# Attention then a squared-ReLU feed-forward layer on one core: the second batch weighs v in float32, w_out is converted in pieces of 384 columns, the reciprocal is placed late in its slot, and the conversion of w_in follows another timetable

## The chip, the core and the metric

The kernel runs on one core of a Trainium2 chip. The metric is device time in microseconds (us) of one execution; of each kernel several executions are timed and the median is given. TensorE (PE, with PEld for its weight loads) multiplies matrices, VectorE (DVE) and ScalarE (ACT) work element by element, GpSimd (POOL) does so too, and SyncE (SP) issues the DMA transfers from one queue in order. Each engine takes its own instructions in program order.

## The reference

```python
def _attn_ref(q, k, v, g_q, g_k):                 # batch 8, 12 heads, 448 rows, head width 64
    q_n, k_n = rmsnorm(q, g_q), rmsnorm(k, g_k)   # x / sqrt(mean(x*x) + 1e-6) * g
    scores = 1/sqrt(64) * q_n @ k_n.T
    attn = exp(scores - scores.max(-1))
    attn = attn / (attn.sum(-1) + 1e-9)
    return attn @ v

def _moe_ref(x, w_in, w_out, s, b):               # x: 3584 x 768, w_in: 768 x 2048, w_out: 2048 x 768
    r = maximum(x @ w_in, 0)
    return (s * (r * r) + b) @ w_out              # x is the attention's output, heads side by side
```

w_in and w_out come as float64, the rest of the large inputs as float32.

## The kernel before

**Pairs, chunks and slots.** Two heads of one batch entry make a pair; there are 48 pairs, 6 to a batch (`NP = 6`). A pair has `W = 8` score chunks: for each of its two heads, four chunks of up to 128 keys by 448 queries. A hand-written loop runs over slots `s_`, from `FIRST = -22` on, and in slot `s_` the engines get, in a fixed order: the two score matmuls of chunk `s_` (`score_t`, L405 and L408), its exponential on ACT (`exponent`), the jobs that a table lists for this slot (`at(slot, function, ...)`), a score matmul for chunk `s_ + 10` that is only there to find the row maxima (`score`, L367, and on DVE `maximum`, L378), and the weighing of v with chunk `s_ - 2` (`weigh`, L464). All engines are ordered by this loop (`manual_schedule`). Slots below 0 are the prologue, slots 0 to 47 the first batch, 48 to 95 the second, and so on to 383.

**float32 and fp32r.** Matmuls on float32r operands go through PE in one pass. To keep precision an operand is split in a high part (rounded to fp32r, by a cast on ACT) and a low part (the remainder, by a subtraction), and products of parts are added up. For the first batch (`p < NP`) `weigh` instead multiplies plain float32: the exponential is written to a float32 tile `e` (L420) and one float32 matmul with `vf` does the chunk, without any split. For the other pairs the exponential stays in PSUM (L424), `split_e` casts it to `ah` (L432, ACT), `split_e_lo` subtracts to `al` (L445, DVE), `split_v` splits v (L297 on ACT, L298 on POOL), and a chunk takes three matmuls, or two where the fourth key chunk of 64 rows packs both parts in one tile: 22 for the 8 chunks of a pair.

**Filler.** From the end of slot 60 on the feed-forward matmuls of the batch before (`ffn_in`, L180: 16 units of 18) stand between the score matmuls, 6 to a slot (`FILL`), so that each batch of 48 slots carries 288 of them. At each change of batch, in slots 48*b + 11 to 48*b + 13, `split_x` splits the six x tiles of the batch just finished (L513 on ACT, L514 on DVE).

**Per pair besides.** `scale` and `split_kq` prepare q and k of the pairs from 6 on (L329, L351, L352 on POOL, L330 on DVE). `take` moves the weighed values out of PSUM, `gather` brings the row sums by DMA into `zt`, `divide` step 0 (slot `8p + 13`) adds 1e-9 and takes the reciprocal on DVE (L489, L490), steps 1 and 2 spread it by DMA, step 3 multiplies on POOL (L505).

**The weights.** `load_double` makes the two parts of a float64 piece: a DMA into `w64`, four integer or float operations on DVE (L125, L128, L130, L133) that put a float32 word together in `wa`, a square on ACT (L126) that serves one of them, a cast of the high part on ACT (L136) and the subtraction of the low part on POOL (L139). w_in has 24 pieces of 128 x 512. `PACE` lists the slot in which each piece's conversion starts, and a piece takes five slots; two pieces are loaded ahead, and the load of a further one stands three slots after each start:

```python
PACE = (-18, -10, *range(1, 61, 5), *range(61, 91, 3))
at(s_ + n, convert, n)      # n = 0..4; convert stands behind the slot's other DVE work
at(s_ + 3, load_piece)
```

**The last stage.** After the slots come the last batch's feed-forward units and the conversion of w_out, 48 pieces of 128 x 256 (`WO = 256`), in a loop over `m` with three pieces a step; a step's casts and subtractions follow four steps later, since w_out takes over w_in's buffers quarter by quarter. `squares` loads three tiles of 128 rows of relu values (1 MB each), squares them on ACT (L682), scales them on DVE (L683) and splits them (L687 ACT, L688 DVE); `ffn_out` multiplies them with w_out (L700), the first three tiles together, then one by one. A PSUM bank of a feed-forward unit comes free when ACT's relu (L197, `rectify`) has read it, and the first three output tiles need six such banks. SP is ordered by the scheduler there, and `ffn_out` as well.

## Time and profile before

| | |
|---|---|
| median of 3 runs | 1547.24 us (1546.6 to 1549.03) |
| profiled execution | 1545.13 us, of which the span from the first to the last instruction is 1543.3 us |
| busy share of the span | PE 95%, PEld 87%, DVE 58%, ACT 53%, POOL 49% |
| mean granted TensorE clock | 0.979 |
| DMA | 230.86 MB, mean 150 GB/s |
| chain that ended last | PE 29%, DVE 3%, DMA 2% of the span (the rest of the span is not in it) |

PE is busy nearly all of the time on the average, but not in every stage: the page's 40 slices show PE between 0.6 and 0.9 in the first seven of them and dips again about two thirds of the way. The views to read are therefore those by stage: the busy time of each engine in a stretch, the waits in it, and the order of instructions in time.

### The profile page before, as it was taken

Reading aid. Unit: us, or ns where it says so; the run is one execution under the profiler, and the core shown is the slowest. Engines: PE = TensorE matmul, PEld = TensorE weight load, DVE = VectorE, ACT = ScalarE, POOL = GpSimd, SP = SyncE. Lnnn points to the kernel's source line nnn. Section 1 sums busy time; section 2 is a strip of 40 time slices with the busy share of each in tenths; the row PEclk is TensorE's granted clock in tenths of the full one; section 3 lists DMA queues with packets and bytes.
Section 4 is the critical chain, followed back from the end, with each engine's and each line's share of the span. In section 5 each row is a group of like instructions: output and inputs, shape, how many; then the busy total and the mean of one; then the engine's idle time right before and its main releaser. Section 6 shows DMA issues by size and latency. Waiting matters only on the chain. (4 is left out here: it accounts for less than half of the span.)

```text
span 1543.3 us, 21847 instructions
## 1 busy us (share of the span) xinstructions
PE 1459.3 (95%) x7380; PEld 1343.6 (87%) x7380; DVE 892.6 (58%) x1399; ACT 812.5 (53%) x1522; POOL 748.6 (49%) x611
## 2 busy tenths in 40 slices
PE   7886799999999999999999999997899999999998
PEld 6654688899899899899889889996899999999998
DVE  5989998766666766766666664389532222222210
ACT  4766676666666666766766666346342222222210
POOL 6799898777667667667677753135500000000000
PEclk8998899999999999999999999998899999999999
DMA  4477676566566566656666651466243323323300
GB/s 118 133 198 217 183 231 201 161 193 202 159 189 191 173 193 193 183 166 201 189 172 194 188 164 56 125 218 199 82 140 91 97 75 88 101 76 86 103 21 31
DMA packets 218751, 230.86 MB, mean 150 GB/s; under 512 B 72912, under 2 KB 193744, under 8 KB 218640
## 3 DMA queue, kind: packets, MB, share of 16 engines
q1 hardware_dynamic: 218640, 229.47, 50.3%
q8 instruction: 58, 0.95, 0.3%
q14 instruction: 53, 0.43, 0.1%
HBM read 177.21 MB, written 40.84 MB: 141 GB/s over the span
## 5 line engine op out<-in xcount | busy, mean ns | idle before, releaser
L180 PE MATMUL ph<-x,wih 128*128 128x448 f32 x1536 | 493.1, 368 | 0.0
L424 ACT ACTIVATE st<-st 128x448 f32<-128x448 f32 x336 | 176.5, 525 | 261.2 <-PE st L408 244.6
L180 PEld LDWEIGHTS ph<-x,wih 128*128 128x128 f32 x1536 | 290.8, 189 | 24.0 <-issue 0.2
L378 DVE TENSOR_REDUCE nmx<-sh 112x1 fp32r<-112x448 f32 x384 | 237.1, 620 | 126.4 <-PE sh L367 121.1
L180 PE MATMUL ph<-x,wil 128*128 128x448 f32 x768 | 282.2, 367 | 0.0
L700 PE MATMUL po<-woh,gh 128*128 128x384 f32 x896 | 230.9, 337 | 12.5 <-ACT gh L687 7.8
L700 PE MATMUL po<-wol,gh 128*128 128x384 f32 x896 | 230.5, 337 | 4.1 <-POOL wol L139 4.1
L700 PE MATMUL po<-woh,gl 128*128 128x384 f32 x896 | 229.1, 336 | 0.0
L464 PE MATMUL av<-ah,vs 128*128 128x448 f32 x672 | 194.7, 371 | 6.1 <-DVE ah L445 3.2
L445 DVE TENSOR_TENSOR al<-st,ah 128x448 fp32r<-128x448 f32 x252 | 155.5, 617 | 44.6 <-ACT ah L432 26.0
L432 ACT CAST ah<-st 128x448 fp32r<-128x448 f32 x336 | 179.6, 535 | 2.0
L700 PEld LDWEIGHTS po<-woh,gh 128*128 128x128 f32 x896 | 163.4, 189 | 13.9 <-ACT gh L687 8.1
L367 PE MATMUL sh<-ka,qa 128*112 128x448 f32 x384 | 147.8, 387 | 23.0 <-POOL ka L351 8.4
L700 PEld LDWEIGHTS po<-wol,gh 128*128 128x128 f32 x896 | 163.4, 189 | 5.5 <-POOL wol L139 5.5
L700 PEld LDWEIGHTS po<-woh,gl 128*128 128x128 f32 x896 | 162.9, 189 | 0.5 <-DVE gl L688 0.5
L405 PE MATMUL st<-qa,ka 128*128 128x448 f32 (+1 forms) x384 | 159.2, 414 | 0.5 <-ACT e L420 0.5
L180 PEld LDWEIGHTS ph<-x,wil 128*128 128x128 f32 x768 | 145.2, 189 | 11.4
L351 POOL TENSOR_TENSOR ka<-kq,ka 64x448 fp32r<-64x448 f32 x84 | 100.4, 1196 | 108.4 <-ACT ka L348 97.3
L464 PEld LDWEIGHTS av<-ah,vs 128*128 128x128 f32 x672 | 127.5, 191 | 20.3 <-DVE al L445 3.5
L408 PE MATMUL st<-qb,kb 128*128 128x448 f32 (+1 forms) x384 | 142.4, 371 | 0.0
L682 ACT ACTIVATE r<-r 128x2048 f32<-128x2048 f32 x28 | 53.7, 1917 | 168.2 <-DMA r<-r_d 168.2
L367 PEld LDWEIGHTS sh<-ka,qa 128*112 128x112 f32 x384 | 107.7, 281 | 36.0 <-POOL ka L351 9.9
(75 smaller groups left out, 2099.1 us busy)
## 6 DMA issues: line engine op xcount, KB each, us to landing
kq<-in_dram SPq DMA_DIRECT2D x84, 448.0 KB, 4.8
rb<-i_d SPq DMA_DIRECT2D x84, 448.0 KB, 5.5
r_d<-r SPq DMA_DIRECT2D x128, 224.0 KB, 2.0
r<-r_d SPq DMA_DIRECT2D x24, 1024.0 KB, 5.8
raw<-in_dram SPq DMA_DIRECT2D x42, 448.0 KB, 4.7
w64i<-in_dram SPq DMA_DIRECT2D x24, 512.0 KB, 4.8
w64o<-in_dram SPq DMA_DIRECT2D x48, 256.0 KB, 3.1
kb<-ka SPq DMA_DIRECT2D x96, 112.0 KB, 3.4
```

What stands on the lines that cost most here:

```text
L180: T.matmul(ph[:, :SEQ], w[:, cc, f0 : f0 + P], xs[b, cc][:, part, :], start=n == 0, stop=n == 3 * NCC - 1,)
L351: G.tensor_tensor(ka[n][D:, a], t[D:, 0], ka[n][D:, a].bitcast(F32), ALU.subtract)
L367: T.matmul(sh[:QC, :SEQ], qa[p % 2][:, a].rearrange("k (p c) -> k c p", c=NQ)[:, c], ka[p % 2][:, a], start=True, stop=True,)
L378: V.tensor_reduce(out=nmxs[p][:, c : c + 1], in_=sh[:QC, :SEQ], op=ALU.max, axis=AX.X, negate=True)
L405: T.matmul(st[:rows, :SEQ], ka[n][:, keys], qa[n][:, q], start=True, stop=False)
L408: T.matmul(st[:rows, :SEQ], kb[n][:, keys], qb[n][:, q], start=False, stop=True,)
L424: S.activation(st[:rows, :SEQ], st[:rows, :SEQ], AF.Exp)
L432: S.copy(ah[:rows], sts[i][0][:rows, :SEQ])
L445: V.tensor_tensor(al, st[:rows, :SEQ], ah[:rows].bitcast(F32), ALU.subtract)
L464: T.matmul(av[:, :SEQ], x, a, start=kc == 0 and m == 0, stop=kc == 3 and m == len(todo) - 1,)
L682: S.activation(r, r, AF.Square)
L700: T.matmul(po[e][0][:, :HALF], x[:, fc, :], w[:, f, e * HALF : (e + 1) * HALF], start=fc == 0 and m == 0, stop=fc == NFC - 1 and m == 2,)
```

## The change

It has five parts.

1. `NV = 2 * NP` takes the place of `NP` where float32 or split is chosen: pairs 6 to 11 (the second batch) too use the float32 `e` and `vf`. `load_v` for them is two DMAs, later by four slots, with two memsets on POOL.
2. `PACE` converts five pieces of w_in in the prologue (slots -18, -14, -10, -6, -2), one in slot 2, and from slot 6 on one in five slots, to slot 91.
3. The reciprocal (`invert`) is put in the group of jobs that stand behind the slot's other DVE work, with `convert`.
4. w_out goes in 32 pieces of 384 columns, two a step; the subtraction of the low part is on DVE (`rest=V`) and not on POOL. The relu and the casts of the older pieces stand one step earlier among the four parts of a loop step.
5. The loads of `squares` no longer stand ahead of the loop, but in its steps 1, 2 and 3; its other parts come one step earlier.

```diff
-PACE = (-18, -10, *range(1, 61, 5), *range(61, 91, 3))
+PACE = (-18, -14, -10, -6, -2, 2, *range(6, 92, 5))
...
+    NV = 2 * NP
...
-    WO = 256
+    WO = 384
...
-        G.tensor_tensor(dst_lo, af, dst_hi.bitcast(F32), ALU.subtract)
+        (rest or G).tensor_tensor(dst_lo, af, dst_hi.bitcast(F32), ALU.subtract)
...
         def load_v(p):
-            if p < NP:
+            if p < NV:
...            # the same in chunk, exponent, split_e, split_e_lo, weigh
+        def invert(p):
+            zt = zts[p]
+            V.tensor_scalar(zt, zt, 1e-9, None, ALU.add)
+            V.reciprocal(zt, zt)
+
         def divide(p, step):
-            if step == 0:
-                zt = zts.pop(p)
-                V.tensor_scalar(zt, zt, 1e-9, None, ALU.add)
-                V.reciprocal(zt, zt)
-                zts[p] = zt
-            elif step == 1:
+            if step == 1:
...
+        late = (convert, invert)
...
-            at(s0 - (9 if p >= NP else 5), load_v, p)
-            if p >= NP:
+            at(s0 - (9 if p >= NV else 5), load_v, p)
+            if p >= NV:
                 at(s0 - 3, split_v, p)
-            at(s0 + 13, divide, p, 0)
+            at(s0 + 13, invert, p)
...
                 for f, a in jobs[s_]:
-                    if f is convert:
+                    if f in late:
                         f(*a)
...
-                w = op.tile([P, WO, 2], I32, tag="w64", bufs=5, name=f"w64o{i}")
-                a = op.tile([P, WO], I32, tag="wa", bufs=16, name=f"wao{i}")
-                m = op.tile([P, WO], F32, tag="wm", bufs=3, name=f"wmo{i}")
-                yield load_double((w, lambda a=a: a, m), *part)
+                w = op.tile([P, WO, 2], I32, tag="w64", bufs=4, name=f"w64o{i}")
+                m = op.tile([P, WO], F32, tag="wm", bufs=2, name=f"wmo{i}")
+
+                def words(i=i):
+                    return op.tile([P, WO], I32, tag="wa", bufs=10, name=f"wao{i}")
+
+                yield load_double((w, words, m), *part, apart=True, rest=V)
...
-            todo = list(islice(pieces, 3))
-            for g in chain(todo, first):
+            todo = list(islice(pieces, 2))
+            for g in todo:
                 next(g)
-            for m in range(NFC + NFC // NS):
+            for m in range(NFC + later_by):
...
-                now, todo = todo, list(islice(pieces, 3))
+                now, todo = todo, list(islice(pieces, 2))
                 for g in todo:
                     next(g)
-                old = waiting[:3] if m >= NFC // NS else []
+                if m in (1, 2, 3):
+                    next(first[m - 1])
+                old = waiting[:2] if m >= later_by else []
...
-                    if step == 1:
+                    if step == 0:
                         rectify()
                         keep_r()
-                    if step == 2:
                         for g in old:
                             for _ in range(GAP):
                                 next(g)
+                    if step == 2:
+                        for g in old:
+                            next(g)
                 waiting += now
+                if m in (6, 8, 10):
+                    next(first[(m - 6) // 2])
                 if m in (7, 9, 11):
-                    next(first[(m - 7) // 2])
-                if m in (8, 10, 12):
-                    gs.append(next(first[(m - 8) // 2]))
+                    gs.append(next(first[(m - 7) // 2]))
...
-    vs[: n // b, : p // 2, 3] = 0
+    vs[: 2 * n // b, : p // 2, 3] = 0
```

What the change does to the order is shown at three places. Each kernel has its own line numbers: in the kernel after, a line's number is one to six higher, and that of the two `zt` lines one lower.

The prologue on DVE. `nmx` is the row maximum of score chunk `sh`, `ka` and `qb` are the split of turned k and q rows, `ssq` the sum of squares of rows, `wai` a piece of w_in. Before:

```order
L378 TENSOR_REDUCE nmx0_337<-sh4_384 112x1
L378 TENSOR_REDUCE nmx0_337<-sh5_403 112x1
L378 TENSOR_REDUCE nmx0_337<-sh6_413 112x1
L257 TENSOR_TENSOR ka1_185<-tk1_0_0_393,ka1_185 64x448
L258 SCALAR_TENSOR_TENSOR qb1_191<-tk1_0_1_398,gqk_200,qa1_187 64x448
L233 TENSOR_REDUCE ssq2_0_418<-sq2_0_409 112x8
L378 TENSOR_REDUCE nmx0_337<-sh7_420 112x1
L378 TENSOR_REDUCE nmx1_431<-sh8_429 112x1
```

The same stretch of the kernel after:

```order
L379 TENSOR_REDUCE nmx0_346<-sh4_394 112x1
L126 TENSOR_SCALAR wai3_398<-w64i3_336 128x512
L129 SCALAR_TENSOR_TENSOR wai3_398<-w64i3_336,wai3_398 128x512
L379 TENSOR_REDUCE nmx0_346<-sh5_417 112x1
L131 SCALAR_TENSOR_TENSOR wai3_398<-w64i3_336,wai3_398 128x512
L379 TENSOR_REDUCE nmx0_346<-sh6_428 112x1
L134 SCALAR_TENSOR_TENSOR wai3_398<-wih0_242,wai3_398 128x512
L258 TENSOR_TENSOR ka1_185<-tk1_0_0_407,ka1_185 64x448
L259 SCALAR_TENSOR_TENSOR qb1_191<-tk1_0_1_412,gqk_200,qa1_187 64x448
L234 TENSOR_REDUCE ssq2_0_434<-sq2_0_424 112x8
L379 TENSOR_REDUCE nmx0_346<-sh7_438 112x1
L379 TENSOR_REDUCE nmx1_450<-sh8_448 112x1
```

The four operations of piece 3 have come in here; those of piece 2 stand where piece 1 stood, piece 1 ahead of the first `ka`, and piece 4 between the maxima of chunks 8 and 11.

The change of batch on DVE, slots 108 and 109: `x` is the split of x, `al` and `ah` the low parts of the exponentials, `zt` the reciprocal. Before:

```order
L445 TENSOR_TENSOR ah107_3118<-st107_3083,ah107_3118 64x448
L378 TENSOR_REDUCE nmx14_2963<-sh118_3130 112x1
L309 TENSOR_REDUCE ssq17_3150<-raw17_3014 128x14
L489 TENSOR_SCALAR zt12_2954<-zt12_2954 128x7
L490 RECIPROCAL zt12_2954<-zt12_2954 128x7
L330 SCALAR_TENSOR_TENSOR kq15_1_3037<-kq15_1_3037,gqk_200,rb15_1_3039 128x448
L514 TENSOR_TENSOR x1_4_3162<-u10_2840,x1_4_3162 128x448
L514 TENSOR_TENSOR x1_5_3165<-u11_3061,x1_5_3165 128x448
L445 TENSOR_TENSOR al108_3174<-st108_3113,ah108_3147 128x448
L378 TENSOR_REDUCE nmx14_2963<-sh119_3168 112x1
```

After:

```order
L446 TENSOR_TENSOR ah107_2908<-st107_2873,ah107_2908 64x448
L379 TENSOR_REDUCE nmx14_2753<-sh118_2920 112x1
L310 TENSOR_REDUCE ssq17_2940<-raw17_2804 128x14
L331 SCALAR_TENSOR_TENSOR kq15_1_2827<-kq15_1_2827,gqk_200,rb15_1_2829 128x448
L515 TENSOR_TENSOR x1_4_2950<-u10_2627,x1_4_2950 128x448
L515 TENSOR_TENSOR x1_5_2953<-u11_2851,x1_5_2953 128x448
L446 TENSOR_TENSOR al108_2962<-st108_2903,ah108_2937 128x448
L379 TENSOR_REDUCE nmx14_2753<-sh119_2956 112x1
L488 TENSOR_SCALAR zt12_2744<-zt12_2744 128x7
L489 RECIPROCAL zt12_2744<-zt12_2744 128x7
```

The two `zt` instructions have gone behind `al` and the maximum; the split of x is where it was.

The last stage on DVE, loop step 4: `wao` is a piece of w_out, `wol` the low part of a quarter. Before, three pieces, and the low parts are on POOL:

```order
L125 TENSOR_SCALAR wao12_11117<-w64o12_11116 128x256
L125 TENSOR_SCALAR wao13_11120<-w64o13_11119 128x256
L125 TENSOR_SCALAR wao14_11123<-w64o14_11122 128x256
L128 SCALAR_TENSOR_TENSOR wao12_11117<-w64o12_11116,wao12_11117 128x256
L128 SCALAR_TENSOR_TENSOR wao13_11120<-w64o13_11119,wao13_11120 128x256
L128 SCALAR_TENSOR_TENSOR wao14_11123<-w64o14_11122,wao14_11123 128x256
L130 SCALAR_TENSOR_TENSOR wao12_11117<-w64o12_11116,wao12_11117 128x256
L130 SCALAR_TENSOR_TENSOR wao13_11120<-w64o13_11119,wao13_11120 128x256
L130 SCALAR_TENSOR_TENSOR wao14_11123<-w64o14_11122,wao14_11123 128x256
L133 SCALAR_TENSOR_TENSOR wao12_11117<-wmo12_11118,wao12_11117 128x256
L133 SCALAR_TENSOR_TENSOR wao13_11120<-wmo13_11121,wao13_11120 128x256
L133 SCALAR_TENSOR_TENSOR wao14_11123<-wmo14_11124,wao14_11123 128x256
```

After, two pieces and two low parts of the pieces of step 0:

```order
L126 TENSOR_SCALAR wao8_10919<-w64o8_10871 128x384
L126 TENSOR_SCALAR wao9_10922<-w64o9_10873 128x384
L129 SCALAR_TENSOR_TENSOR wao8_10919<-w64o8_10871,wao8_10919 128x384
L129 SCALAR_TENSOR_TENSOR wao9_10922<-w64o9_10873,wao9_10922 128x384
L131 SCALAR_TENSOR_TENSOR wao8_10919<-w64o8_10871,wao8_10919 128x384
L131 SCALAR_TENSOR_TENSOR wao9_10922<-w64o9_10873,wao9_10922 128x384
L140 TENSOR_TENSOR wol0_10719<-wao0_10751,woh0_10718 128x384
L140 TENSOR_TENSOR wol0_10719<-wao1_10754,woh0_10718 128x384
L134 SCALAR_TENSOR_TENSOR wao8_10919<-wmo8_10872,wao8_10919 128x384
L134 SCALAR_TENSOR_TENSOR wao9_10922<-wmo9_10874,wao9_10922 128x384
```

The subtractions have come from POOL into the middle of DVE's step, and they wait for ACT's casts of the same two pieces.

More of the change, by code (lines that the diff above doesn't have):

```diff
@@ L113, in psum, with load_double @@
         return ps.tile([P, 512], F32, tag=bank, name=name), bank
-    def load_double(room, dst_hi, dst_lo, src, apart=False):
+    def load_double(room, dst_hi, dst_lo, src, apart=False, rest=None):
         w, words, m = room
@@ L394, in chunk @@
             j, kc = divmod(g, NKC)
-            return p, j, kc, P if kc < 3 or p < NP else REST
+            return p, j, kc, P if kc < 3 or p < NV else REST
         def score_t(i):
@@ L416, in exponent @@
             st, bank = sts[i]
-            if p < NP:
+            if p < NV:
                 e = ap.tile([P, SEQ], F32, tag="ah", bufs=3, name=f"e{i}")
@@ L427, in split_e @@
             p, j, kc, rows = chunk(i)
-            if p < NP:
+            if p < NV:
                 return
@@ L435, in split_e_lo @@
             p, j, kc, rows = chunk(i)
-            if p < NP:
+            if p < NV:
                 return
@@ L455, in weigh @@
             moved = movers.pop(i)
-            if p < NP:
+            if p < NV:
                 of = vrs[p].rearrange("p c u d -> p c (u d)")
@@ L645, in attention_then_relu2_ffn @@
                 for f, a in jobs[s_]:
-                    if f is convert:
+                    if f in late:
                         f(*a)
@@ L716, in attention_then_relu2_ffn @@
         pieces = pieces()
-        n = 3 * NFC // NS
+        later_by = NFC // NS
         with tc.manual_schedule(engines=ORDERED - {ENGINE.SP}):
             waiting = []
-            todo = list(islice(pieces, 3))
-            for g in chain(todo, first):
+            todo = list(islice(pieces, 2))
+            for g in todo:
                 next(g)
-            for m in range(NFC + NFC // NS):
+            for m in range(NFC + later_by):
                 if m < NFC:
```

## The prediction

> **What bounds the kernel now.** I read the busy time by stage first, since the averages (PE 95%) hide it. The columns are: stretch, its length, busy time (and instructions) of PE, PEld, DVE, ACT, POOL, then granted clock, DMA share and GB/s. The second fence counts the L408 matmuls, one per slot.
>
> ```profile
> 0.00:34.20 34.20, 25.27 (x163) 23.44 (x164) 17.53 (x30) 12.05 (x20) 23.23 (x31) 0.87 0.42 123
> 20.00:34.20 14.20, 7.98 (x35) 6.39 (x36) 12.65 (x23) 7.35 (x13) 10.05 (x11) 0.69 0.42 120
> 34.20:127.00 92.80, 78.15 (x301) 53.05 (x301) 80.69 (x125) 64.07 (x124) 76.73 (x69) 0.96 0.62 173
> 127.00:156.80 29.80, 20.70 (x69) 15.17 (x69) 28.88 (x43) 19.06 (x40) 28.77 (x23) 0.84 0.69 201
> 156.80:260.60 103.80, 90.32 (x418) 79.05 (x418) 100.36 (x146) 72.68 (x148) 90.30 (x63) 0.96 0.67 202
> 260.60:279.70 19.10, 19.10 (x96) 17.54 (x95) 12.69 (x21) 12.83 (x27) 13.59 (x11) 1.00 0.66 198
> 279.70:302.50 22.80, 19.93 (x96) 17.39 (x95) 17.23 (x28) 15.90 (x33) 14.93 (x12) 1.00 0.50 153
> 398.20:422.50 24.30, 21.45 (x96) 18.51 (x95) 17.91 (x28) 15.91 (x33) 15.84 (x13) 0.93 0.48 146
> 993.00:1099.00 106.00, 89.41 (x444) 82.42 (x442) 88.81 (x201) 54.78 (x120) 44.52 (x36) 0.93 0.67 206
> 1099.00:1543.00 444.00, 440.24 (x2524) 439.52 (x2524) 103.70 (x76) 102.56 (x76) 8.83 (x13) 0.99 0.28 80
> ```
>
> ```profile
> 127.00:156.80 29.80, 5.17 (x12) 0.84 0.69 201
> 156.80:260.60 103.80, 13.60 (x36) 0.96 0.67 202
> ```
>
> So the second batch is 29.8 us for slots 48 to 59, which have no filler yet, and 103.8 us for slots 60 to 95. There DVE is busy 97% of the time, and POOL 97% and 87%; PE is not the bound. From 260.6 on eight slots take 19.1 us with PE at 100%: 96 matmuls, 0.20 us each. Batch changes take 22.8 and 24.3 us for the same eight slots. In the last stage (993 to 1099) DVE is busy 84% and PE waits. After 1099 PE is full, and nothing there is changed. The change can move only the stages ahead of 1099.
>
> What PE waits for in the second batch (total, times, longest), and then in the last stage:
>
> ```profile
> PE av L464 <- DVE al L445: 17.1, 10, 3.3
> ```
>
> ```profile
> PE po L700 <- ACT gh L687: 7.8, 1, 7.8
> PE po L700 <- POOL wol L139: 4.1, 2, 3.6
> PE po L700 <- ACT r L197: 3.1, 2, 1.6
> PE po L700 <- ACT woh L136: 1.7, 1, 1.7
> ```
>
> **Prologue.** DVE at the place where pieces 1 (before) and 2 (after) stand:
>
> ```profile
> 22.82 0.42 DVE L125 TENSOR_SCALAR wai<-w64i 128x512 int32<-128x512 int32 x1
> 23.27 0.69 DVE L128 SCALAR_TENSOR_TENSOR wai<-w64i,wai 128x512 int32<-128x512 int32 x1
> 24.42 0.68 DVE L130 SCALAR_TENSOR_TENSOR wai<-w64i,wai 128x512 int32<-128x512 int32 x1
> 25.55 0.68 DVE L133 SCALAR_TENSOR_TENSOR wai<-wih,wai 128x512 f32<-128x512 f32 x1
> ```
>
> A piece costs DVE 0.42 + 0.69 + 0.68 + 0.68 = 2.5 us. Piece 1 goes ahead of the first `ka`, before 20 us, where DVE is busy 17.53 - 12.65 = 4.9 us of 20: free. Piece 2 takes its old place. Piece 3 (2.5 us) and three quarters of piece 4 (1.8 us) come new between the maxima ahead of slot 0, where DVE is busy 12.65 of 14.2 us. That is 4.3 us of work against 1.55 us of gaps that lie in its own waits for PE: +4.0 us, between +2.8 (all gaps filled) and +9 (ACT's and POOL's steps of both pieces on the path as well). The three loads that come earlier stand on SP ahead of a `kb` or `qb` move each; DMA is at 0.42 there, so I give them nothing, with the +9 as bound. From slot 2 to slot 46 both kernels convert ten pieces.
>
> **float32 in the second batch.** It takes away, for each of 48 chunks, one DVE subtraction and one ACT cast, and for each of six pairs the split of v (first row in the second batch, second at 324 to 400, third over the run):
>
> ```profile
> L445 DVE TENSOR_TENSOR al<-st,ah 128x448 fp32r<-128x448 f32 x36 | 22.1, 613 | 0.7 <-ACT ah L432 0.6
> ```
>
> ```profile
> L445 DVE TENSOR_TENSOR al<-st,ah 128x448 fp32r<-128x448 f32 x24 | 14.9, 619 | 4.5 <-PE av L464 2.8 <-ACT ah L432 1.7
> ```
>
> ```profile
> L298 POOL TENSOR_TENSOR vs<-vr,vs 128x512 fp32r<-128x512 f32 x42 | 54.7, 1303 | 109.1 <-issue 97.4 <-ACT vs L297 10.7 <-POOL qb L352 1.0
> ```
>
> That is 48 x 0.613 = 29 us of DVE and 6 x 1.3 = 8 us of POOL, where two short memsets a pair come in. Pieces started in slots 60 to 95 fall from ten to seven, each 2.5 us of DVE: -7.5 us. It adds PE time. The float32 chunk in the first batch:
>
> ```profile
> 95.51 0.37 PE L367 MATMUL sh<-ka,qa 128*112 128x448 f32 x1
> 95.71 0.91 PE L464 MATMUL av<-e,vf 128*128 128x448 f32 x2
> 96.87 0.47 PE L367 MATMUL sh<-ka,qa 128*112 128x448 f32 x1
> ```
>
> A slot there is 1.36 us from `sh` to `sh`, three one-pass matmuls and this chunk: 1.36 - 0.60 = 0.76 us. The split took 22/8 x 0.20 = 0.55 us, so +0.21 us a chunk, 10 us in all. A filled slot then has nine one-pass matmuls and one chunk: 9 x 0.20 + 0.76 = 2.56 us.
>
> Slots 60 to 95: PE 36 x 2.56 = 92 us. DVE: 100.4 less 36 x 0.613 less 7.5 = 71 us. POOL: 90.3 less 6.5 (five splits) less three low parts of w_in, plus memsets: under 86 us. So PE becomes the bound. The batch change at slot 60 stays (the rows above give 22.8 - 19.1 = 3.7 us for one), and some 3 us for pieces that collide: 98.8 us, -5.0, between -11 (PE alone) and 0 (POOL's chain keeps it).
>
> Slots 48 to 59: PE needs 12 x 1.36 = 16 us, DVE 28.9 - 12 x 0.613 = 22 us, POOL 28.8 - 1.3 = 27.5 us. POOL is now the bound, but its durations hold collisions. The same instruction in the second batch, and at 302 to 398:
>
> ```profile
> L351 POOL TENSOR_TENSOR ka<-kq,ka 64x448 fp32r<-64x448 f32 x13 | 18.5, 1420 | 4.9 <-ACT ka L348 2.3 <-DVE nmx L378 1.8
> ```
>
> ```profile
> L351 POOL TENSOR_TENSOR ka<-kq,ka 64x448 fp32r<-64x448 f32 x10 | 11.5, 1152 | 14.3 <-ACT ka L348 12.6 <-DVE nmx L378 1.4
> ```
>
> At 1152/1420 of its time POOL would need 22 us; at its present time 27.5. I take 26: -3.8, between -7.5 and -2.
>
> The Trainium skill (SBUF — State Buffer, "Who interferes with whom") says that a DVE instruction with at most one SBUF input, outside its two-port modes, does not contend with GpSimd, and one with two SBUF inputs does. `al` has one input in PSUM; that it lasts 613 ns beside a crowded POOL and 619 beside a free one agrees. By the rule its removal relieves POOL of nothing, this term would be -2.3, and the sum 1.5 us higher.
>
> **Reciprocal, late.** In slot 109 the order on DVE was `zt`, then the split of x, then `al`, for which PE waits:
>
> ```profile
> 295.89 0.16 DVE L489 TENSOR_SCALAR zt<-zt 128x7 f32<-128x7 f32 x1
> 296.09 0.20 DVE L490 RECIPROCAL zt<-zt 128x7 f32<-128x7 f32 x1
> 299.24 0.47 PE L464 MATMUL av<-al,vs 128*128 128x448 f32 x1 [1.88 <-DVE al L445]
> ```
>
> Behind `al` it gives back 0.16 + 0.20 us at each of six changes: -2.2 us. Three of six changes have the clock of the row at 398.2 (0.93 of 24.3 us, 1.7 us lost); a shorter wait may spare one: -3 in all, between -2 and -7. In the first batch DVE stood waiting in this instruction:
>
> ```profile
> DVE zt L489 <- DMA zt<-uz: 12.8, 4, 5.6
> ```
>
> Behind it stood `kq` and the maximum; now it stands behind them, and only SP's next DMAs and POOL's `u` wait for it. Between 0 and -12.8; POOL (83% busy) limits these slots, and of its work only the first pair's split of v goes: -2.
>
> **The last stage.** DVE's work on w_out, from these rows:
>
> ```profile
> 998.30 1.09 DVE L128 SCALAR_TENSOR_TENSOR wao<-w64o,wao 128x256 int32<-128x256 int32 x3
> 999.30 1.09 DVE L130 SCALAR_TENSOR_TENSOR wao<-w64o,wao 128x256 int32<-128x256 int32 x3
> 1006.72 0.29 DVE L125 TENSOR_SCALAR wao<-w64o 128x256 int32<-128x256 int32 x1 [5.32 <-DMA w64o<-in_dram]
> 1042.54 1.34 DVE L683 TENSOR_SCALAR r<-r,sb_s,sb_b 128x2048 f32<-128x2048 f32 x1
> 1049.07 2.28 DVE L688 TENSOR_TENSOR gl<-r,gh 128x2048 fp32r<-128x2048 f32 x1
> ```
>
> Three take 1.00 us undisturbed, 0.33 each; with L125 (0.2) a piece of 256 is 1.2 us, 48 are 58. For 384 columns I put 0.47 (an estimate between these 0.33 and the 0.6 from one to the next at 512) and 0.28: 1.7 us, 32 are 54. The subtraction is new on DVE: 2.28/2048 x 384 + 0.05 = 0.47, 32 are 15. The three tiles cost 3 x (1.34 + 2.28) = 11 in both. So 80 against 69 us of work; but DVE was busy 88.8 us in the stage, of which 3 for x, so 17 were collisions with POOL's subtractions, which end. The 5.32 us wait for loads came of two tiles of 1 MB that SP issued ahead of the pieces; they now come behind. DVE's idle time was 17.2 us; keeping 10 of it, the conversion ends near 993 + 3 + 80 + 10 = 1086, some 11 earlier. PE's waits (16.7 us, and 0.07 x 106 = 7.4 us of clock) hang on loop steps 8 to 13 (relu of the banks, `gh`), 60% of the way: -6, between -24 (all) and +12 (no gap filled, each of 12 steps waiting some 1 us for ACT's casts).
>
> **Sum.** 4.0 - 2 - 3.8 - 5.0 - 3 - 6 = -15.8 us. The profiled execution took 1545.1 us (span 1543.3), 2.1 below the median; its sum is 1529.3, and against the median of 1547.2 it is 1531.4.
>
> **Rivals.** *The cover is gone, the gain is not there* (1544): PE's waits in the last stage are set by the order in which relu, squares and loads come, not by the conversion (0), the second batch gains what POOL leaves (-2 and -3), first batch and batch changes give 1 each: 4 - 1 - 2 - 3 - 1 = -3. For it: POOL at 97%, and a wait of 7.8 us on `gh`. Against: 17 us of waits for L445 in the second batch that cannot come back.
>
> *The last stage becomes load-bound* (1555): its loads are the same 12.6 MB of w_out, 3.7 MB of relu written and some 4 MB read, 20 MB; at the 206 GB/s of its row that is 99 us, more than DVE's 80. At 160 GB/s it is 128 us: 22 longer than now, of which PE sees most, +20 for the -6 above. It is slower than before from a stage of 119 us on (172 GB/s). Against: DMA share 0.67, and fewer, larger transfers.
>
> *PE never waits in the last stage* (1516): quarters, squares and banks all come ahead; -21 for -6. For it: PE's 16.7 us are six waits, and four of them (12.6 us) hang on ACT, which is busy half the time. Against: the first two tiles still need loop step 11.
>
> **Chances.** Forecast 0.64 (1525 to 1538), gain not there 0.17, load-bound 0.06, no wait 0.13. A measurement of this kernel tells about 0.2% (3.1 us) from no change. Faster: 0.64 + 0.13 + half of the 0.17 = 0.85; same 0.08; slower 0.06 + 0.01. The range 1518 to 1544 leaves out the load-bound case and most of the no-wait case.
>
> **What would show it.** Slot 0 near 38 us, not 34; slots 48 to 59 in 26 us with POOL over 95%; slots 60 to 95 in 99 us with PE over 95% and no wait for L445; batch changes near 22.4 us; no POOL work after the second batch's changes but that of pairs; DVE's last low part near 1086 and PE idle 12 us at most in the last stage. I am wrong if the prologue costs over 9 us, if POOL keeps slots 60 to 95 over 103 us, or if DVE's new subtraction waits for ACT.

## The result and the profile after

The kernel after takes 1505.12 us in the median (1504.26 to 1506.17), the kernel before 1547.2 in the same comparison: a ratio of 0.9726, 95% interval 0.971 to 0.9743. It is 42 us faster where 16 were forecast, and the time lies below the range. The profiled executions have spans of 1504.4 and 1543.3 us, 38.9 apart. A slot begins with its L408 matmul (L409 after), and by these starts the 38.9 us are put to the stages (a minus is time saved):

| stage | forecast | measured, before to after |
|---|---|---|
| prologue, to slot 0 | +4.0 | +3.1 (34.3 to 37.4 us) |
| first batch, slots 0 to 47 | -2 | +4.2 (92.8 to 97.0) |
| slots 48 to 59 | -3.8 | -5.5 (29.8 to 24.3) |
| slots 60 to 95 | -5.0 | -7.3 (103.8 to 96.5) |
| six batch changes, slots 96 to 383 | -3 | -10.2 (711.3 to 701.1) |
| from slot 383 to the end | -6 | -23.3 (571.3 to 548.0) |

The page's first part and its slices of the clock show that PE went from 95% to 97% and POOL from 49% to 46%:

```profile
PE 1452.9 (97%) x7344; PEld 1330.3 (88%) x7344; DVE 874.7 (58%) x1319; ACT 786.3 (52%) x1436; POOL 689.9 (46%) x569
PEclk8898999999999999999999999999999999999999
```

The busy time by stage of the kernel after, in the columns of the prediction's first fence (stretch, length, PE, PEld, DVE, ACT, POOL, clock, DMA share, GB/s):

```profile
20.00:37.30 17.30, 8.01 (x35) 6.43 (x36) 16.47 (x28) 9.36 (x17) 12.44 (x12) 0.64 0.55 159
37.30:55.10 17.80, 14.70 (x53) 10.40 (x53) 15.67 (x24) 10.92 (x21) 10.93 (x12) 0.78 0.41 114
55.10:134.30 79.20, 66.31 (x250) 44.68 (x249) 71.83 (x104) 53.91 (x104) 63.89 (x61) 0.96 0.66 181
134.40:158.70 24.30, 19.24 (x62) 12.43 (x61) 22.21 (x34) 12.38 (x25) 23.46 (x18) 0.93 0.76 208
158.70:255.20 96.50, 93.94 (x391) 74.57 (x390) 72.22 (x96) 52.98 (x103) 80.09 (x67) 0.98 0.73 214
274.80:296.60 21.80, 19.95 (x96) 17.37 (x95) 16.54 (x28) 15.80 (x33) 15.37 (x11) 1.00 0.54 167
392.30:414.10 21.80, 19.94 (x96) 17.38 (x95) 16.58 (x28) 15.80 (x33) 15.44 (x11) 1.00 0.58 169
977.00:1060.00 83.00, 82.98 (x431) 78.52 (x431) 74.35 (x156) 48.08 (x81) 0.00 (x0) 1.00 0.81 260
1060.00:1504.40 444.40, 439.97 (x2539) 439.65 (x2537) 112.21 (x91) 105.78 (x84) 0.00 (x0) 1.00 0.28 80
```

In slots 60 to 95 (158.70 to 255.20) PE is now busy 97% of the time and DVE 75%: there PE is the bound. A batch change takes 21.8 us at full clock both times, where before it took 22.8 or, with clock lost, 24.3. In the last stage (977 to 1060) PE is busy 82.98 of 83 us, POOL has no work, and the DMAs move 260 GB/s where 206 were moved before. Two rows of DVE's timeline (start, duration, instruction) of the kernel after bound its work on w_out; the third is POOL's last on w_out in the kernel before, with 15 low parts:

```profile
980.88 0.36 DVE L126 TENSOR_SCALAR wao<-w64o 128x384 int32<-128x384 int32 x1 [3.29 <-DMA w64o<-in_dram]
1062.20 3.83 DVE L140 TENSOR_TENSOR wol<-wao,woh 128x384 fp32r<-128x384 f32 x8
```

```profile
1093.99 13.84 POOL L139 TENSOR_TENSOR wol<-wao,woh 128x256 fp32r<-128x256 f32 x15 [2.23 <-ACT woh L136]
```

The last low part is done at 1066.0, 109.7 us behind slot 383; before, the last on POOL was done at 1107.8, 135.9 us behind it. The four waits of PE for this stage that the prediction quoted have no successor: in the stretch 975 to 1085 no wait of PE is left. Of the waits of the other engines there, the longest is now one in which ACT waits for PE:

```profile
ACT gh L693 <- PE po L706: 14.0, 2, 12.1
```

### The profile page after: what moved, and what is told of

It is laid out like the page before. It is cut to its first block, busy times and chain, and to the rows that moved or that the text cites. A ratio compares the mean times of both kernels' runs of the same rounds, so it can differ in the third digit from the quotient of the medians.

```text
span 1504.4 us, 21397 instructions
## 1 busy us (share of the span) xinstructions
PE 1452.9 (97%) x7344; PEld 1330.3 (88%) x7344; DVE 874.7 (58%) x1319; ACT 786.3 (52%) x1436; POOL 689.9 (46%) x569
## 4 chain that ended last, share of the span: by engine, by line
PE 88%; DVE 5%; DMA 3%; issue 1%; ACT 1%; POOL 1%; SPq 0%; DVEq 0%; POOLq 0%; ACTq 0%
PE po L706 31%; PE ph L181 30%; PE av L465 13%; PE st L406 4%; PE st L409 4%; PE sh L368 4%; DVE x L515 2%; PE warmth L272 1%; DVE nmx L379 1%; DMA zt<-uz 1%; DMA z_d<-zt 1%; DMA rb<-i_d 0%; DVE al L446 0%; DVE wai L134 0%; DVE wai L129 0%
## 5 line engine op out<-in xcount | busy, mean ns | idle before, releaser
L181 PE MATMUL ph<-x,wil 128*128 128x448 f32 x768 | 294.1, 383 | 0.0
L425 ACT ACTIVATE st<-st 128x448 f32<-128x448 f32 (+1 forms) x288 | 151.1, 525 | 220.8 <-PE st L409 204.2
L465 PE MATMUL av<-ah,vs 128*128 128x448 f32 x576 | 164.3, 366 | 0.1
L406 PE MATMUL st<-qa,ka 128*128 128x448 f32 (+1 forms) x384 | 163.5, 426 | 0.5 <-ACT e L421 0.5
L181 PEld LDWEIGHTS ph<-x,wil 128*128 128x128 f32 x768 | 144.4, 188 | 17.8 <-issue 6.9
L433 ACT CAST ah<-st 128x448 fp32r<-128x448 f32 (+1 forms) x288 | 154.1, 535 | 1.8
L446 DVE TENSOR_TENSOR al<-st,ah 128x448 fp32r<-128x448 f32 x216 | 132.1, 611 | 35.6 <-ACT ah L433 21.7
L368 PEld LDWEIGHTS sh<-ka,qa 128*112 128x112 f32 x384 | 107.6, 281 | 42.5 <-ACT wih L137 15.8
L409 PE MATMUL st<-qb,kb 128*128 128x448 f32 (+1 forms) x384 | 141.4, 368 | 0.0
L689 DVE TENSOR_SCALAR r<-r,sb_s,sb_b 128x2048 f32<-128x2048 f32 x28 | 37.6, 1345 | 173.0 <-ACT r L688 173.0
```

The source lines that it names most:

```text
L181: T.matmul(ph[:, :SEQ], w[:, cc, f0 : f0 + P], xs[b, cc][:, part, :], start=n == 0, stop=n == 3 * NCC - 1,)
L368: T.matmul(sh[:QC, :SEQ], qa[p % 2][:, a].rearrange("k (p c) -> k c p", c=NQ)[:, c], ka[p % 2][:, a], start=True, stop=True,)
L406: T.matmul(st[:rows, :SEQ], ka[n][:, keys], qa[n][:, q], start=True, stop=False)
L409: T.matmul(st[:rows, :SEQ], kb[n][:, keys], qb[n][:, q], start=False, stop=True,)
L425: S.activation(st[:rows, :SEQ], st[:rows, :SEQ], AF.Exp)
L433: S.copy(ah[:rows], sts[i][0][:rows, :SEQ])
```

## The parts, one at a time

Each of four kernels is the kernel before with one part of the change. Stages are compared with the profiled execution of before, from slot start to slot start. Their unchanged stages come out up to 4.1 us apart from it, so a stage difference below that size counts as shown only where several profiles have it; the times of the whole kernel are medians, with intervals.

**The last stage alone** (parts 4 and 5 of the change):

```diff
-    WO = 256
+    WO = 384
-        G.tensor_tensor(dst_lo, af, dst_hi.bitcast(F32), ALU.subtract)
+        (rest or G).tensor_tensor(dst_lo, af, dst_hi.bitcast(F32), ALU.subtract)
...                     # and the new buffers and loop over m, all of it
```

> The kernel before with the last stage alone changed (parts 4 and 5). Theory: PE's waits and its lost clock in the last stage go entirely, as in the kernel after, whatever came before: 23 us less, 1524 us, ratio 0.985. Rival, the forecast's term: the waits shrink only as the conversion ends earlier, 6 us, 1541 us.

Measured: 1525.8 us, ratio 0.9865 (0.9851 to 0.988). From slot 383 to the end it takes 548.2 us, as the kernel after does, 23.2 less than before. PE's busy time in the stage, and its only wait there:

```profile
997.40:1103.40 106.00, 105.84 (x564) 101.38 (x563) 87.34 (x172) 55.78 (x92) 0.00 (x0) 1.00 0.68 215
```

```profile
PE po L703 <- ACT r L197: 0.2, 1, 0.2
```

The gain of the last stage comes whole from these two parts, whatever happens in the slots ahead. Its size is less sure than the tenths suggest: the three kernels below, whose last stage is that of before, take 567.2 to 568.8 us there and not 571.3, so it is 19 to 23 us.

**float32 in the second batch alone** (part 1):

```diff
+    NV = 2 * NP
-            if p < NP:
+            if p < NV:
...                     # the same in the other places
```

> The kernel before with float32 v in the second batch alone (part 1). Theory: DVE was the bound of the second batch, so taking 22 us of subtractions from it makes PE the bound even with the old timetable of w_in: the second batch falls from 133.6 to 124 us, 1537 us in all. Rival: the pieces of w_in at three slots' distance keep DVE and POOL the bound: 129 us, 1543 us in all.

Measured: 1530.64 us, ratio 0.9896 (0.9881 to 0.9911). Slots 48 to 95 take 10.7 us less, most of the 12.8 of the whole change; slots 96 to 383 are at +0.8, so none of the gain at the batch changes is its work.

**The timetable alone** (part 2):

```diff
-PACE = (-18, -10, *range(1, 61, 5), *range(61, 91, 3))
+PACE = (-18, -14, -10, -6, -2, 2, *range(6, 92, 5))
```

> The kernel before with the timetable of w_in alone (part 2). Theory: slot 48 comes 7 to 9 us later, as in the kernel after, and the second batch, bound by DVE, gives back the three pieces (7.5 us of DVE): 1546 to 1549 us. Rival: POOL or the subtractions keep the second batch as long as it was: 1555 us.

Measured: 1543.68 us, ratio 0.9981 (0.9971 to 0.999). Slot 0 comes 3.4 us later, slot 8 7.5 later, slot 48 7.5; the second batch gives 6.0 back.

**The late reciprocal alone** (part 3):

```diff
-            at(s0 + 13, divide, p, 0)
+            at(s0 + 13, invert, p)
-                    if f is convert:
+                    if f in late:
...                     # the second place, and the function invert
```

> The kernel before with the reciprocal alone moved (part 3). Theory: each of six changes of batch loses 1.0 us of PE's wait (0.36 us of the two instructions, 0.65 us because the scaling of kq no longer meets POOL), and the three losses of clock of 1.6 us go: 10 us less, 1537 us; the first batch stays within 2 us. Rival, the forecast's term: 0.36 us a change and one clock spared: 3 to 4 us less, 1544 us, the rest of what the kernel after gained there coming from elsewhere.

Measured: 1528.36 us, ratio 0.9879 (0.9863 to 0.9896). Slots 96 to 383 take 10.7 us less: the whole gain at the batch changes. Its first batch takes 2.0 less, which one profile does not show; of the five kernels with the old table of w_in the three with the early reciprocal take 91.7 to 92.8 us there, the two with the late one 90.8 and 90.3 (the second of these stands further below), so some 2 us are its work. Two of its changes, at full clock like the other four:

```profile
279.30:301.10 21.80, 19.95 (x96) 17.38 (x95) 16.60 (x28) 15.78 (x33) 15.39 (x11) 1.00 0.54 165
396.80:418.60 21.80, 19.95 (x96) 17.36 (x95) 16.60 (x28) 15.78 (x33) 15.40 (x11) 1.00 0.57 169
```

The four medians lie 21.1, 16.3, 3.3 and 18.6 us below the 1546.94 of before in these runs, 59.3 together for 42 of the whole change. Two overlaps are seen: float32 and the timetable relieve the same slots (10.7 and 6.0 us alone, 12.8 together), and each of the last three kernels shows 2.5 to 4.1 us less in the last stage, which none of them changes. If the one profile of before is long by that much there, it is counted again in the first's 23.2; that is argued, not shown.

## Why PE no longer waits in the last stage

Four kernels take one thing back from the kernel after, all in the last stage.

**The subtraction back on POOL:**

```diff
-                yield load_double((w, words, m), *part, apart=True, rest=V)
+                yield load_double((w, words, m), *part, apart=True)
```

> The kernel after with the subtraction of w_out's low parts back on POOL, all else of the last stage as after. Theory: POOL's subtractions collide with DVE's and each end late, so PE waits again: 10 to 20 us more than after, 1515 to 1525 us. Rival: what freed PE is the order of the loads, relu and casts and the larger pieces; taking 15 us of work from DVE does no harm: within 3 us of after, 1505 us.

Measured: 1520.03 us, ratio 0.9822 (0.9807 to 0.9836); 15.1 us of the last stage's 23.3 are gone. DVE's rows for w_out (count, then busy us and mean ns, then idle time ahead of it) in the stretch 970 to 1100, first of the kernel after, then of this one:

```profile
L134 DVE SCALAR_TENSOR_TENSOR wao<-wmo,wao 128x384 f32<-128x384 f32 x32 | 16.3, 550 | 0.0
L140 DVE TENSOR_TENSOR wol<-wao,woh 128x384 fp32r<-128x384 f32 x32 | 16.1, 550 | 0.0
L126 DVE TENSOR_SCALAR wao<-w64o 128x384 int32<-128x384 int32 x32 | 10.3, 355 | 8.6 <-DMA w64o<-in_dram 8.6
```

```profile
L134 DVE SCALAR_TENSOR_TENSOR wao<-wmo,wao 128x384 f32<-128x384 f32 x32 | 20.4, 673 | 0.0
L129 DVE SCALAR_TENSOR_TENSOR wao<-w64o,wao 128x384 int32<-128x384 int32 x32 | 19.5, 649 | 0.0
L131 DVE SCALAR_TENSOR_TENSOR wao<-w64o,wao 128x384 int32<-128x384 int32 x32 | 18.7, 624 | 0.0
L126 DVE TENSOR_SCALAR wao<-w64o 128x384 int32<-128x384 int32 x32 | 16.0, 528 | 10.6 <-DMA w64o<-in_dram 7.8 <-POOL wol L140 2.7
```

```profile
L140 POOL TENSOR_TENSOR wol<-wao,woh 128x384 fp32r<-128x384 f32 x32 | 55.7, 1769 | 50.0 <-ACT woh L137 45.7 <-DVE wao L129 4.3
```

In the kernel after L129, L131 and L134 take 16.3 us each, so the four operations are 3 x 16.3 + 10.3 = 59.2 us; with POOL beside them the same 128 instructions take 74.6. The subtraction costs DVE 16.1 us when DVE does it and 15.4 us when POOL does it, and POOL takes 1769 ns for what DVE does in 550. DVE gains nothing by handing it over, and the detour over a second engine is added. PE feels the detour. Rows of this kernel's waits from 976 on, and then one of the kernel after (975 to 1085):

```profile
PE po L706 <- ACT r L198: 11.9, 2, 7.5
ACT wmo L127 <- DVE wao L134: 29.2, 15, 4.9
```

```profile
ACT wmo L127 <- DVE wao L134: 9.1, 5, 2.4
```

ACT's squares (L127) wait for the buffer `wm` that DVE's L134 frees, 29.2 us in place of 9.1 (27.4 in the kernel before); the relu (L198) stands behind them on ACT, and PE's first output tiles need the banks that the relu frees. Twice ACT's timeline of this run shows the whole chain: squares that have waited 4.90 and 4.67 us for DVE, a relu right behind them at 1041.13 and 1054.65, and a wait of PE that ends at 1041.71 and 1055.22. A change that moves the relu alone was not tried.

**Three more steps back, one kernel each: the loads of `squares` ahead of the loop, pieces of 256 columns (three a step), and the old places of relu and casts in a step:**

```diff
-            for g in todo:
+            for g in chain(todo, first):
...                     # and no loads in steps 1, 2 and 3
```

```diff
-    WO = 384
+    WO = 256
-            todo = list(islice(pieces, 2))
+            todo = list(islice(pieces, 3))
...                     # three for two wherever pieces are taken, and as many bytes of buffers
```

```diff
-                    if step == 0:
+                    if step == 1:
                         rectify()
                         keep_r()
...                     # and the casts of the older pieces in step 2
```

> The kernel after with the loads of squares ahead of the last stage's loop again, as before. Theory: two tiles of 1 MB stand in front of the pieces of step 1, DVE waits some 5 us more at the start, and since PE had no slack left the wait is passed on in part: 3 to 8 us more than after, 1508 to 1513 us. Rival: the conversion catches up, PE sees nothing of it: 1505 us.

> The kernel after with w_out in 48 pieces of 256 columns, three a step, with the same bytes of buffers. Theory: DVE works 48 x 1.54 = 74 us instead of 32 x 2.13 = 68 us on w_out, 6 us more over 16 steps, of which PE sees some: 2 to 6 us more than after, 1507 to 1511 us. Rival: the size of a piece is most of the gain: 15 us more, 1520 us.

> The kernel after with relu and the casts of the older pieces where they stood before, one or two of the four parts of a step later. Theory: DVE reaches its subtractions before ACT's casts are done and waits in every step, 0.5 to 1 us in 12 steps: 5 to 10 us more, 1510 to 1515 us. Rival: ACT has time enough, nothing changes: 1505 us.

Measured: 1507.54 (1504.77 to 1508.6), 1505.86 (1504.7 to 1506.34) and 1505.09 us (1502.0 to 1505.27); in the profiles the time from slot 383 on is 1.7, 2.6 and 0.1 us longer than after's. None of the three has a ratio apart from the kernel after's (0.9744, 0.973 and 0.9721, each +-0.0016 or less). The waits that come back are short, one fence for each of the first two:

```profile
PE po L706 <- ACT r L198: 1.4, 1, 1.4
```

```profile
PE po L706 <- ACT r L198: 1.1, 1, 1.1
PE po L706 <- ACT woh L137: 0.6, 1, 0.6
```

So 15 of the 23 us hang on the engine of the subtraction, and none of the other three steps, taken back by itself, costs more than 3. That pieces of 256 and the loads' old place bring waits of 1 to 2 us back at once says how narrow the margin is. The remaining 8 us are not assigned: the step by which squares and `gh` come earlier in the loop was not taken back by itself, nor several steps together.

## The timetable and the reciprocal again

Four kernels start from the kernel after. Three change `PACE` alone, one puts the inversion back.

```diff
-PACE = (-18, -14, -10, -6, -2, 2, *range(6, 92, 5))
+PACE = (-18, -10, *range(1, 61, 5), *range(61, 91, 3))      # the old table
```

> The changed kernel with the old table PACE; all its other parts stay. Theory A (an early piece costs what it takes; with float32 in place the second batch no longer needs the three pieces that were moved ahead): the +7.4 us up to slot 48 that the new table alone cost go, and the second batch loses only 12.8 - 10.7 = 2.1 us: 1505.1 - 7.4 + 2.1 = 1500, slot 0 near 34 us. Theory B (the three pieces are worth in the second batch what they were worth without float32, 6.1 us): 1505.1 - 7.4 + 6.1 = 1504, no difference that can be told.

```diff
+PACE = (-18, -14, *range(1, 61, 5), *range(61, 91, 3))      # second piece at -14
```

> The changed kernel with the old table, but for the second piece, which goes from slot -10 to -14, ahead of the first ka, where DVE is idle for most of the time. Theory A: a piece there is free and one between the maxima ahead of slot 0 costs DVE 2.5 us: 1 to 2 us below the run with the old table, 1498 to 1499. Theory B: the maxima ahead of slot 0 wait for loads and for PE, not for the piece: same as with the old table.

```diff
+PACE = (-18, -14, *range(1, 50, 6), 54, *range(59, 93, 3))  # fewer early
```

> The changed kernel with the second piece at -14, eight from slot 1 to 49 (every six slots), then thirteen, eleven of them in slots 60 to 95 and nearly all three slots apart. Two pieces fewer stand in the first batch, two more in the second. Theory A (first batch bound by DVE and POOL, 2.3 us a piece; second bound by PE, a piece there hidden): another 3 to 4 us, 1495. Theory B (a piece costs the same wherever it stands once DVE and POOL are over 75% busy): as the run with the piece at -14; the second batch gives back in slots 48 to 95 what the first gains.

```diff
-                    if f in late:
+                    if f is convert:
...                     # the same at the second place
```

> The changed kernel with the inversion of zt back at its old place, ahead of the maximum, kq and al in its slot. Theory A (the batch changes' 1.0 us each and the half-speed windows of the clock come of this order alone): +10 us at the six changes and +2 to +3 in the first batch, 1517. Theory B (the gain at the changes came of float32 in the second batch and of other timing as well): +2 to +4, 1508.

Measured, with slot starts in us (the kernel after: 37.4, 134.4 and 255.2):

| kernel | time, us | ratio to before | slot 0 | slot 48 | slot 96 |
|---|---|---|---|---|---|
| old table | 1499.28 | 0.9696 (0.9681 to 0.971) | 34.2 | 124.5 | 247.2 |
| second piece at -14 | 1495.21 | 0.9669 (0.9653 to 0.9685) | 30.1 | 119.0 | 243.6 |
| fewer early | 1493.6 | 0.9662 (0.9647 to 0.9676) | 30.3 | 116.6 | 242.2 |
| inversion not late | 1518.78 | 0.9823 (0.9808 to 0.9837) | 37.0 | 136.8 | 256.7 |

The old table is better than the new one by some 5 us once the second batch has float32 (5.8 by the medians, 4.6 by the ratios to before; the two kernels were not timed side by side): 9.8 us are saved up to slot 48, and the second batch needs 122.7 us in place of 120.8. Theory A said 1500. The three pieces were sent ahead to relieve slots that another part of the change had relieved.

With the second piece at -14 slot 0 comes 4.1 us earlier than with the old table, more than the 1 to 2 expected. The windows of this kernel:

```profile
0.00:20.00 20.00, 16.29 (x130) 15.98 (x131) 8.17 (x13) 6.71 (x11) 13.27 (x20) 1.00 0.44 136
20.00:30.10 10.10, 5.95 (x35) 4.82 (x34) 9.55 (x18) 5.19 (x10) 8.45 (x11) 0.95 0.51 142
```

The piece lies in the first 20 us, where DVE is busy 8.17, and the maxima follow each other with DVE at 95%. Between 20 us and slot 0 DVE has 18 instructions in place of the 23 of before, and the granted clock is 0.95 in place of 0.69. Part of the 4.1 us is the start, which differs between profiles: this kernel's first `ka` begins at 18.34, that with the old table at 19.69, and it begins between 18.40 and 19.86 in the five profiles whose prologue is that of before. From there to slot 0 these five take 13.4 to 14.5 us, this kernel takes 11.8. The float32 kernel, whose `ka` begins at 18.40 with the old table, has slot 0 at 31.8 and a clock of 0.86: against it the piece at -14 is worth 1.7 us, as expected.

Two pieces fewer in the first batch go with 86.2 us for it (slots 0 to 47) in place of 88.9, and the second batch gives back 1.0. The change of slots 104 to 111 takes 2.7 us more, though its reciprocal is late. DVE's split of x lasts 2.10 us there (1.16 in the kernel after), PE waits for the `al` behind it, and the clock falls to 0.93:

```profile
278.68 2.10 DVE L515 TENSOR_TENSOR x<-u,x 128x448 fp32r<-128x448 f32 x2
```

```profile
281.38 0.47 PE L465 MATMUL av<-al,vs 128*128 128x448 f32 x1 [1.99 <-DVE al L446]
```

The time, 1493.6, cannot be told from 1495.21: the run does not decide between the theories. These two are the fastest kernels of this study, 0.7% below the kernel after.

With the inversion at its old place the batch changes are as slow as in the kernel before, and four of six, not three, lose clock. A change that does and one that does not:

```profile
276.30:300.60 24.30, 21.42 (x95) 18.60 (x94) 17.87 (x28) 15.78 (x33) 16.64 (x14) 0.93 0.55 159
875.00:897.80 22.80, 19.92 (x96) 17.38 (x95) 17.31 (x28) 15.85 (x33) 15.29 (x12) 1.00 0.50 156
```

The slots 96 to 383 take 12.3 us more than in the kernel after, for the 10 of theory A: what the late inversion gains at the changes it gains by itself, with float32 or without. The first batch takes 2.8 more, as theory A said, but four other kernels with the new table and the late inversion lie between 92.5 and 97.4 us there, so this run alone does not show it.

## Why the prediction was wrong

**The step that failed most is the last stage's term, -6 for -23.3.** Its pieces of work were right: 0.47 us an operation, 15 for the subtraction, 17 of collisions that end. Measured are 0.47 from start to start, 16.1 and, with POOL put back, 15.4. DVE's conversion was due to end some 11 us earlier and ended 15.9 earlier, counted from slot 383. What failed is the last sentence, "60% of the way": PE's waits were taken to shrink in proportion to how far the loop had come. In the runs they went whole, because every input that had ended a wait came earlier by more than all the waits up to it. Rows of PE's timeline show where the waits stood; before:

```profile
1051.05 0.44 PE L700 MATMUL po<-woh,gh 128*128 128x384 f32 x1 [1.50 <-ACT r L197]
1063.07 0.69 PE L700 MATMUL po<-woh,gh 128*128 128x384 f32 x1 [7.76 <-ACT gh L687]
1065.32 0.69 PE L700 MATMUL po<-woh,gh 128*128 128x384 f32 x1 [1.56 <-ACT r L197]
...
1098.92 0.69 PE L700 MATMUL po<-wol,gh 128*128 128x384 f32 x1 [3.64 <-POOL wol L139]
```

and the first output matmul of the kernel after:

```profile
1033.57 0.51 PE L706 MATMUL po<-woh,gh 128*128 128x384 f32 x2
```

The first output matmul starts 77 us behind slot 383 in both kernels (1049.2 before); every wait lies behind it, so a lead is worth something only there, and there all of it counts, since each wait delays the next. The second tile's `gh` (the high part of its squared values) ended the longest wait. Its cast, before and after:

```profile
1061.12 1.90 ACT L687 CAST gh<-r 128x2048 fp32r<-128x2048 f32 x1
```

```profile
1025.87 1.92 ACT L693 CAST gh<-r 128x2048 fp32r<-128x2048 f32 x1
```

That is 89.1 and 69.5 us behind slot 383: 19.6 earlier, and done 6 us ahead of PE's first output matmul. Of the 19.6 one loop step comes of the new place in the code; the rest comes of shorter steps, 16 of which lie between the first and the last relu of the loop, 991.6 to 1093.1 before and 975.9 to 1058.5 after (6.3 and 5.2 us each). The low part that ended PE's last wait, at 1098.9 or 126.9 us behind slot 383, is done 104.6 us behind it in the kernel after, 22.3 earlier. Both leads exceed the 16.7 us of waits, so PE keeps all of them, and the clock lost with them: 16.7 + 7.4 = 24 was the bound "(all)". The margin was small: the matmul of the last wait now runs 21.0 us earlier, 1.4 us behind its low part. By the prediction's own 1086, 21.8 us ahead of the last low part on POOL (1107.8), the term would have been all of the 16.7 at least. The rival in which PE never waits (1516, with 0.13) is what happened in this stage; it named the order of quarters, squares and banks as the reason, and the runs show the engine of the subtraction as the larger part. (The load-bound rival's 1555 is counted from the profiled execution, the other two from the median; from the median it is 1557.)

**The batch changes, -3 for -10.2.** The moved instructions were priced at their own duration, 0.16 + 0.20 us. The wait they stood in shrank by 1.0. POOL's and DVE's rows at the first change, of the kernel before:

```profile
295.92 1.15 POOL L329 TENSOR_TENSOR kq<-kq,rb 128x448 f32<-128x448 f32 x1
296.21 1.35 DVE L330 SCALAR_TENSOR_TENSOR kq<-kq,gqk,rb 128x448 f32<-128x448 f32 x1
```

and of the kernel after, with the matmul that had waited 1.88 us:

```profile
290.92 2.72 POOL L330 TENSOR_TENSOR kq<-kq,rb 128x448 f32<-128x448 f32 x1
290.89 0.68 DVE L331 SCALAR_TENSOR_TENSOR kq<-kq,gqk,rb 128x448 f32<-128x448 f32 x1
293.23 0.47 PE L465 MATMUL av<-al,vs 128*128 128x448 f32 x1 [0.86 <-DVE al L446]
```

Before, POOL had begun 0.29 us ahead of DVE, and DVE's instruction took 1.35 us; now DVE begins first, takes 0.68, and POOL's takes 2.72, which nobody waits for. That is 0.36 + 0.67 us at each change. The Trainium skill (SBUF — State Buffer, "Who interferes with whom") says that the port pair which the two engines share is an exclusive lock, and that the order of issue decides who blocks; these two pairs of rows agree. The profiles of the fourteen kernels hold 84 such changes. Where POOL had begun 0.2 to 0.3 us ahead (30 of them) DVE's instruction takes 1.34 to 1.42 us; where DVE is ahead by 0.01 to 0.04 (53) it takes 0.67 or 0.68. The one left is that of the run with fewer early pieces: DVE was ahead by 0.32, its split of x was the long one, and the wait was 1.99 us again. The second part is the clock: three changes had lost 1.5 us each (24.3 for 22.8), of which the prediction spared one. Their waits are down from 1.9 to 0.9 us and none loses any: 6 x 1.0 + 3 x 1.5 = 10.5.

**The first batch, -2 for +4.2.** The reciprocal's share was right, as far as the five profiles with the old table show it. What was left out is the rest of the early pieces: they were counted up to slot 0, and "from slot 2 to slot 46 both kernels convert ten pieces" hid that the pieces begun ahead of slot 0 end behind it. Slots 0 to 7 take 17.8 us for 13.2, with 24 DVE instructions for 22, one of which lasts 2.22 us where the prediction's row had 0.68, and with PE waiting:

```profile
39.55 2.22 DVE L134 SCALAR_TENSOR_TENSOR wai<-wih,wai 128x512 f32<-128x512 f32 x1
```

```profile
PE sh L368 <- ACT wih L137: 7.7, 2, 4.6
PE sh L368 <- DVE ka L258: 3.1, 2, 1.7
```

The second fence is of the stretch 30 to 75, in which PE waited 4.5 us for `ka` before and not for `wih`; the prologue's bound with "ACT's and POOL's steps on the path as well" was seen, but one stage too early.

**The second batch, -8.8 for -12.8.** Right in kind: PE 97% in slots 60 to 95, POOL 97% in slots 48 to 59, no wait for L446. Of this 5.5 us fall to slots 48 to 59, for 3.8, and there the reason was wrong. POOL's instructions were to become shorter without `al`; before and after, slots 48 to 59:

```profile
L351 POOL TENSOR_TENSOR ka<-kq,ka 64x448 fp32r<-64x448 f32 x3 | 4.3, 1448 | 0.2
L505 POOL TENSOR_TENSOR u<-uz,zb 64x448 f32<-64x448 f32 x4 | 5.6, 1394 | 0.1
```

```profile
L352 POOL TENSOR_TENSOR ka<-kq,ka 64x448 fp32r<-64x448 f32 x3 | 4.3, 1432 | 0.2
L506 POOL TENSOR_TENSOR u<-uz,zb 64x448 f32<-64x448 f32 x2 | 2.3, 1172 | 0.1
```

`ka` lasts 1448 and 1432 ns. The other rows go both ways: `u` and `qb` became shorter (1394 to 1172 and 1594 to 1433 ns), the low part of w_in and `ri` (the inverse roots of sums of squares) longer (1306 to 1440 and 2592 to 2826). At their old durations the six kinds of work that stay would take 24.2 us, and they take 23.7, so the durations are worth half a microsecond. The stage became shorter because there is less of POOL's work in it: two products `u`, a split of v, a low part of w_in and a short `ri` fewer (23 instructions to 18).

**The prologue, +4.0 for +3.1**, held. From the first `ka` to slot 0 the seven profiles with the new table take 17.9 us, the five with the old one 13.4 to 14.5.

Forecast and measured add up to -15.8 and -38.9: 17.3 of the 23 us between them are the last stage, 7.2 the batch changes, 4.0 the second batch and 0.9 the prologue, against 6.2 the other way in the first batch.

## What to carry to other kernels

Where an engine waits several times, find for each wait the input that ends it: if every such input comes earlier by more than all the waits up to it, the term is all of them, not a share by how far the producer has come. Work on POOL beside DVE was not off the path here, where both read SBUF: price it by what it adds to DVE's durations, and read which of the two began first. Of a change with several parts, ask of each whether another part has already removed what it relieves; here the float32 batch made the early pieces a loss of some 5 us.

## What the runs showed of the hardware

- Handing 32 subtractions to POOL saved DVE 16.1 us of instructions and cost it 15.4 us in its others. An operation with one input in SBUF was hit too: L126 went from 355 to 528 ns on the average.
- A DVE instruction that moved by 0.3 us halved in duration (1.35 to 0.68 us) because it came to stand ahead of POOL's, whose own went from 1.15 to 2.72.
- A wait of 1.9 us of PE, some 7 us behind one of 1.0 us in a stretch that is otherwise full, was followed by 1.5 us of lost clock in three of six batch changes, in four of six with the inversion put back, and in 18 of the 30 in all five kernels with the early reciprocal. With 0.9 us in its place, no clock was lost in any of 53 changes of the nine kernels with the late one; their one wait of 1.99 us lost it. The Trainium skill (TensorE: Matmul & The Clock Gate, "Part 1: The HAM clock gate") puts the fall to half speed behind an idle window of about 3.4 us; the slow window here has that length, but the wait ahead of it was 1.9 us, and the measurement decides. One row of the kernel before shows it:

```profile
417.90:421.30 3.40, 3.40 (x10) 2.77 (x11) 2.22 (x5) 1.44 (x4) 1.45 (x2) 0.50 0.20 39
```
